# The experts' first product of units 8 to 15 as 2x2 blocks with seven products, in a three-stage kernel on one Trainium2 core

## The chip, the core and the metric

The kernel runs on one core of one Trainium2 chip. The core has five engines that run side by side, each through its own instructions in order: TensorE (PE, with the loading of its stationary operand as PEld), VectorE (DVE), ScalarE (ACT), GpSimd (POOL) and SyncE (SP), which here only issues DMAs. Work on one engine waits for another's by semaphores. Matmul results go to PSUM, which PE writes and DVE and ACT read. The metric is device time in microseconds (us), the median of three runs.

## The reference

Three stages, each feeding the next, all in float32 (cut to what is computed):

```python
# 1. attention, 2 x 8 heads, 576 tokens, head size 64: a window of 32 keys, for half
#    the heads at a stride of 4; its output is x, 1152 tokens x 512
# 2. four experts, 512 -> 1024 -> 512
p = domain_probs / (domain_probs.sum(-1) + 1e-9)
for e in range(4):
    h = maximum(x @ w1[e], 0)
    out += p[:, e:e+1] * (h @ w2[e])
# 3. one layer 512 -> 2048 -> 512, its weights given in 64 bits
h = out @ w_in
P = a0 + a1*h + a2*h**2 + a3*h**3
Q = 1 + |b0|*|h| + |b1|*h**2
result = (P / (Q + 1e-6)) @ w_out
```

## The kernel before, in words

**Numbers in two parts.** Every operand of the large products is split in a high part (rounded to the matmul's own float32 form) and a low part (what the rounding lost), and a product is the sum of three: high times high, high times low, low times high.

**Units, chunks, groups.** The 1152 tokens are three chunks of 384 (TC). Hidden features are cut into units of 256; units 0 to 15 are the four experts, units 16 to 23 the last layer. Two units make a group g. An *h step* is the first product of one unit on one chunk: 2 blocks of 128 features, 4 pieces of the inner dimension, 3 products, so 24 matmuls of 128x128 by 128x384 (`h_bank`, line 321), into a PSUM tile of two banks. ACT then writes the relu's high part (`hh`, line 334) and DVE the low part (`hl`, line 335, which reads `hh`). An *o tile* is the second product of a group on 128 tokens: 12 matmuls of 512 columns (`o_half`, line 358) into one PSUM bank, and DVE multiplies it with the expert's weight and adds it to an accumulator in SBUF (`o_sum`, *acc*, line 382). There are three two-bank tiles for h steps, used in turn, and two banks for o tiles, `pso`; a bank is written again when what was in it has been read. The high and low parts of the first product are held in SBUF, six buffers of each.

**Weights.** A unit's w1 and w2 are loaded by SP into one of four raw buffers and split by `split_w` (lines 91 to 109): for each half, ACT casts 128x512 (line 105) and DVE subtracts (line 106). The split tiles come from one pool of four per name.

**Conversion.** Beside this, `convert` (lines 119 to 172) turns the 64-bit words of the last layer's weights into high and low parts, in 32 pieces of 128x512. A piece's words are loaded one piece ahead. ACT first takes a magnitude (line 143); then DVE works in six steps: t (line 145); t again (line 150); e and f (lines 155, 158); f plus t (line 162); a masking of f by the magnitude (line 165), which ACT copies into w (line 168); and the low part w (line 170), which reads ACT's copy, with the store of the piece to DRAM (line 171). The last layer loads from there. A generator yields after each step, and `pump(n)` puts the next n steps into the instruction streams; two sets of buffers alternate.

**Order.** The order of instructions on each engine is the order in which the code issues them; nothing reorders it. Attention comes first, with twelve units interleaved by hand. In the expert layer a group's order is: the h steps of both units on one chunk, then three o tiles; this for the chunks 0, 1, 2, the o tiles being those of the chunk before (of group g - 1 ahead of chunk 1's). Each h step and each o tile is followed by `pump(2)`. The splits and loads of the coming group's weights stand between them: `split_w1` before the h steps of chunk 1, `split_w2` before those of chunk 2. The last layer has no conversion; its activation is a longer chain on ACT and DVE.

Of the kernel before, what the change touches and what calls it, by code (L numbers as in the profile page):

```python
# [33 lines left out]
TC = 384  # L35
# [3 lines left out]
NG1, NG = 2 * E, 2 * E + F2 // 512  # L39
QSCALE = 1.0 / D ** 0.5  # L40
# [4 lines left out]
def body(ctx, tc, qkv, mask, dp, w1, w2, w1d, w2d, coef, out):  # L45
# [5 lines left out]
    wp = ctx.enter_context(tc.tile_pool(name="wp", bufs=4))  # L51
    dram = ctx.enter_context(tc.tile_pool(name="dram", bufs=1, space=DRAM))
    rawp = ctx.enter_context(tc.tile_pool(name="rawp", bufs=4))
# [11 lines left out]
    mask_sb = const.tile([128, 4, 320], BF16, name="mask_sb")  # L65
# [11 lines left out]
    w1s, w2s, scratch = {}, {}, {}  # L77
# [12 lines left out]

    def split_w(store, nm):
        raws = {}

        def split(u, halves=(0, 1)):
            if u >= 2 * NG1:
                return
            if halves[0] == 0:
                raws[u] = store[u]
                store[u] = wp.tile([128, 2, 1024], F32R, tag=nm, name=nm)
            raw, w = raws[u], store[u]  # L100
# [13 lines left out]
    def weight(store, u, n):  # L114

        return (store[u][:, i].rearrange("p (k f) -> p k f", k=n) for i in range(2))


    def convert(pool):
# [15 lines left out]
        for n, (_, dst, s) in enumerate(pieces):  # L135
# [4 lines left out]
            f = pool.tile([128, 512], F32, tag="f", name="f")  # L140
# [198 lines left out]

    def rows(t):  # L340
# [130 lines left out]
    with tc.manual_schedule():  # L471
        attn_pool, x_pool = tc.tile_pool(name="attn", bufs=3), tc.tile_pool(name="psx", bufs=1, space=PSUM)
        ap, psx = attn_pool.__enter__(), x_pool.__enter__()
# [50 lines left out]
        for n, f in enumerate(then):  # L524
# [7 lines left out]
            9: [lambda: split_w2(3), lambda: load_w1(5)],  # L532
# [131 lines left out]
        attn_pool.__exit__(None, None, None)  # L664
        third.append(ctx.enter_context(tc.tile_pool(name="psh3", bufs=1, space=PSUM)))
        conv_pool = tc.tile_pool(name="conv", bufs=2)
        steps = convert(conv_pool.__enter__())
# [6 lines left out]
        def h_step(u, c):  # L674
# [3 lines left out]
            if u < 2 * NG1:  # L678
                h_relu(u, c, ps)
                pump()  # L680
# [27 lines left out]
        for g in range(NG):  # L708
            u = 2 * g
            if g == 0:  # L710
                h_step(0, 2)
                h_step(1, 2)
                o_step(0, 2)
                continue
            more = g + 1 < NG
            if g == NG1:
                for _ in steps:
                    pass
                conv_pool.__exit__(None, None, None)
# [16 lines left out]
            elif g > 1:  # L736
# [4 lines left out]
            if g == 1:  # L741
                load_w2(u + 2)
                load_w2(u + 3)
                extra = {0: [(split_w1, u + 2)], 2: [(split_w1, u + 3)]}
            elif more:
                split_w1(u + 2)
                load_w2(u + 2)
            if g > 1:
                h_step(u, 1)
# [3 lines left out]
            if g > 1 and more:  # L753
                split_w1(u + 3)
                load_w2(u + 3)
            if g > 1:
                h_step(u + 1, 1)
# [3 lines left out]
            if more:  # L761
                split_w2(u + 2)
# [3 lines left out]
            if more:  # L766
                split_w2(u + 3)
# [3 lines left out]
            if g == NG1 - 1:  # L771
                x2_half(0, 0)
                x2_half(0, 1)
# [151 lines left out]
```

## Time and profile before

| | |
|---|---|
| median of three runs | 653.68 us (652.66 to 653.69) |
| profiled execution, its own time | 652.89 us |
| its span, first to last instruction | 650.9 us |
| busy: PE, PEld | 639.6 us (98%), 574.6 us (88%) |
| busy: DVE | 485.0 us (75%) |
| busy: ACT, POOL | 277.7 us (43%), 17.0 us (3%) |
| DMA, mean over the span | 122 GB/s |

The profile is one execution. Busy time of PE counts a matmul from its start to its modelled end, and matmuls overlap in the pipeline, so the time that one costs in a row of them is the distance of two starts, which is less than its listed duration. In the chain of waits, a row is a stretch of work on one engine that the end of the program hung on; the next row is what followed it without anything else coming later. The expert layer goes from about 87 to 420 us, and in it the chain's rows alternate between first products (line 321) and second products (line 358). An "idle time" is time that an engine stood still before an instruction, put down to the event that came last.

### The profile page before, as it was taken

The page shows a single profiled execution, that of the slowest core. Times are in us where ns is not written, and L with a number is a line of the kernel's source. Part 1 is how long each engine was busy: PE and PEld are TensorE (multiplying, and loading weights), DVE is VectorE, ACT ScalarE, POOL GpSimd, SP SyncE. Part 2 cuts the span into 40 slices and gives each one's busy share as a digit, 9 for nine tenths or more (in the row PEclk, how much of TensorE's full clock was granted, in tenths as well). Part 3 has the DMA queues.
Part 4 walks back from the last instruction along what each step waited for, and adds up shares of the span by engine and source line. Part 5 has one row for each costly group of instructions (what it writes and reads, how often), then busy time and mean ns, then how long its engine had stood idle before and what let it go on. Part 6 is the DMA issues. An engine that isn't in the chain of part 4 may idle for free.

```text
span 650.9 us, 9488 instructions
## 1 busy us (share of the span) xinstructions
PE 639.6 (98%) x3838; PEld 574.6 (88%) x3839; DVE 485.0 (75%) x693; ACT 277.7 (43%) x518; POOL 17.0 (3%) x30
## 2 busy tenths in 40 slices
PE   8989999999999999999999999999999999999996
PEld 4878898999999999999999999989999999999985
DVE  6767326867867777777767766436999999999986
ACT  5887412413313323223233232115666555556651
POOL 2311100000000000000000000000000000000000
PEclk9999999999999999999999999999999999999999
DMA  9973011545344444454553572431230330300012
GB/s 293 275 219 104 21 65 47 195 148 172 120 161 149 142 163 137 154 162 115 176 162 102 161 254 93 167 130 38 92 130 1 129 130 2 129 1 1 0 49 97
DMA packets 25707, 79.53 MB, mean 122 GB/s; under 512 B 2720, under 2 KB 3232, under 8 KB 23616
## 3 DMA queue, kind: packets, MB, share of 16 engines
q1 hardware_dynamic: 25376, 78.77, 37.4%
q8 instruction: 30, 0.49, 0.3%
q10 hardware_dynamic: 288, 0.16, 0.1%
q14 instruction: 13, 0.11, 0.0%
HBM read 59.79 MB, written 19.14 MB: 121 GB/s over the span
## 4 chain that ended last, share of the span: by engine, by line
PE 94%; DVE 3%; ACT 2%; issue 0%; DVEq 0%; ACTq 0%
PE ps_h L321 46%; PE ps_o L358 43%; PE ps_v L285 1%; ACT pr L250 1%; PE ps_s L271 1%; PE ps_s L218 1%; PE ps_h L403 1%; PE ps_h L547 1%; PE ps_h L358 0%; DVE u L447 0%; DVE acc L388 0%; DVE u L460 0%; DVE sq L455 0%; DVE sq L452 0%; DVE sq L437 0%
## 5 line engine op out<-in xcount | busy, mean ns | idle before, releaser
L321 PE MATMUL ps_h<-xh,w 128*128 128x384 f32 x1152 | 301.7, 336 | 2.0 <-DVE hl L335 2.0
L358 PE MATMUL ps_o<-w,hh 128*128 128x512 f32 x832 | 224.3, 391 | 0.0
L321 PEld LDWEIGHTS ps_h<-xh,w 128*128 128x128 f32 x1152 | 208.8, 188 | 3.9 <-DVE hl L335 2.2
L321 PE MATMUL ps_h<-xl,w 128*128 128x384 f32 x576 | 192.7, 335 | 0.0
L358 PEld LDWEIGHTS ps_o<-w,hh 128*128 128x128 f32 x832 | 155.1, 188 | 31.1 <-ACT hh L334 0.4
L358 PE MATMUL ps_o<-w,hl 128*128 128x512 f32 x416 | 128.6, 390 | 0.0
L321 PEld LDWEIGHTS ps_h<-xl,w 128*128 128x128 f32 x576 | 108.1, 188 | 1.2
L335 DVE SCALAR_TENSOR_TENSOR hl<-ps_h,hh 128x768 fp32r<-128x768 f32 x48 | 45.9, 957 | 73.2 <-ACT hh L334 73.2
L358 PEld LDWEIGHTS ps_o<-w,hl 128*128 128x128 f32 x416 | 78.0, 188 | 16.9 <-DVE hl L335 0.4
L334 ACT ACTIVATE hh<-ps_h 128x768 fp32r<-128x768 f32 x48 | 39.1, 814 | 120.6 <-PE ps_h L321 120.5
L168 ACT CAST w<-f 128x512 fp32r<-128x512 f32 x32 | 19.9, 621 | 123.6 <-DVE f L165 123.6
L382 DVE SCALAR_TENSOR_TENSOR acc<-ps_o,p_sb,acc 128x512 f32<-128x512 f32 x63 | 47.1, 748 | 11.4 <-PE ps_o L358 11.4
L106 DVE TENSOR_TENSOR w<-raw,w 128x512 fp32r<-128x512 f32 x64 | 42.0, 695 | 0.7 <-ACT w L105 0.6
L170 DVE TENSOR_TENSOR w<-f,w 128x512 fp32r<-128x512 f32 x32 | 22.2, 692 | 22.8 <-ACT w L168 22.8
L441 ACT ACTIVATE ab<-sq,cbias 128x768 f32<-128x768 f32 x24 | 22.6, 944 | 37.2 <-DVE sq L437 37.0
L105 ACT CAST w<-raw 128x512 fp32r<-128x512 f32 x60 | 34.0, 617 | 0.0
L432 ACT ACTIVATE sq<-ps_h 128x768 f32<-128x768 f32 x24 | 19.3, 803 | 32.4 <-PE ps_h L321 32.4
L250 ACT ACTIVATE pr<-pr,mx 128x80 f32<-128x80 f32 (+1 forms) x84 | 29.7, 356 | 6.5 <-DVE mx L243 6.3
L437 DVE SCALAR_TENSOR_TENSOR sq<-sq,absb,ab 128x768 f32<-128x768 f32 x24 | 24.3, 1011 | 3.8 <-ACT ab L433 3.8
L467 DVE TENSOR_TENSOR hl<-u,hh 128x768 fp32r<-128x768 f32 x24 | 22.9, 954 | 5.4 <-ACT hh L464 5.4
L447 DVE SCALAR_TENSOR_TENSOR u<-u,na,ps_h 128x768 f32<-128x768 f32 x24 | 24.3, 1014 | 0.9
L460 DVE SCALAR_TENSOR_TENSOR u<-u,na,sq 128x768 f32<-128x768 f32 x24 | 24.3, 1013 | 0.4
(64 smaller groups left out, 521.0 us busy)
## 6 DMA issues: line engine op xcount, KB each, us to landing
w<-w SPq DMA_DIRECT2D x32, 512.0 KB, 3.6
w<-w SPq DMA_DIRECT2D x16, 1024.0 KB, 5.4
raw<-in_w_dram SPq DMA_DIRECT2D x30, 512.0 KB, 5.9
x<-in_w1d_dram SPq DMA_DIRECT2D x16, 512.0 KB, 5.1
x<-in_w2d_dram SPq DMA_DIRECT2D x16, 512.0 KB, 5.2
out_dram<-acc SPq DMA_DIRECT2D x8, 256.0 KB, 2.2
v<-in_qkv_dram SPq DMA_DIRECT2D x6, 320.0 KB, 6.7
qk<-in_qkv_dram SPq DMA_DIRECT2D x4, 448.0 KB, 5.3
```

Source lines behind the costliest of these rows:

```text
L105: (nc.vector.tensor_copy if early else nc.scalar.copy)(w[:, 0, s], raw[:, s])
L106: nc.vector.tensor_tensor(out=w[:, 1, s], in0=raw[:, s], in1=w[:, 0, s].bitcast(F32), op=ALU.subtract)
L250: nc.scalar.activation(pr[:, j, i], pr[:, j, i], AF.Exp, scale=-1.0, bias=self.mx[:, j, i:i + 1], accum_out=self.total[:, j, i:i + 1],)
L321: nc.tensor.matmul(ps[:, i, :TC], lhsT=a[:, k, f], rhs=b[:, k], start=k + n == 0, stop=k + n == 5,)
L334: nc.scalar.activation(hh, ps[:, :, :TC], AF.Relu)
L335: nc.vector.scalar_tensor_tensor(out=hl, in0=ps[:, :, :TC], scalar=0.0, in1=hh.bitcast(F32), op0=ALU.max, op1=ALU.subtract,)
L358: nc.tensor.matmul(ps, lhsT=a[:, i, tk], rhs=b[:, i], start=v + n == 0, stop=v + n == 6)
L382: nc.vector.scalar_tensor_tensor(out=acc[t], in0=ps, scalar=pe, in1=acc[t], op0=ALU.mult, op1=ALU.add)
L437: nc.vector.scalar_tensor_tensor(out=self.sq, in0=self.sq, scalar=absb[:, 1:2], in1=self.ab, op0=ALU.mult, op1=ALU.add,)
L447: nc.vector.scalar_tensor_tensor(out=self.u1, in0=self.u1, scalar=na[:, 1:2], in1=ps, op0=ALU.add, op1=ALU.mult)
L460: nc.vector.scalar_tensor_tensor(out=self.u1, in0=self.u1, scalar=na[:, 0:1], in1=self.sq, op0=ALU.add, op1=ALU.mult)
L467: nc.vector.tensor_tensor(out=self.hl, in0=self.u1, in1=self.hh.bitcast(F32), op=ALU.subtract)
```

## The change

Units 8 to 15 (groups 4 to 7) compute their first product on chunks 1 and 2 another way; chunk 0 stays an h step. Take the two feature blocks (f) against the two chunks (c), and the inner dimension in two halves (k). That is a product of two 2x2 matrices of blocks, and it is formed with seven block products in place of eight (the scheme of Strassen and Winograd). Each block product is 2 pieces of the inner dimension times 3 products, 6 matmuls of 128x384 as before; a unit's two chunks take 42 of them where they took 48.

What goes with it:

- `sum_w1(u)`: four sums of blocks of w1, on DVE (four 128x256 additions), and their split (a 128x1024 cast on ACT, a 128x1024 subtraction on DVE), into a tile `w1t` of the pool `wp1`.
- `sum_x()`: the four sums of half chunks of x, once, in twelve DVE operations of 128x768 and four casts on ACT, given out two at a time behind o tiles of group 3.
- `Blocks`: the products accumulate in the four banks of two h tiles, `c11`, `m`, `c12`, `p`. After the first product ACT writes its negation into `m` (line 441), and after the second ACT copies `p` to SBUF (line 444). `half` (line 450) and `most` (line 461) are two DVE operations of 128x384 that read `m` and the copy and write the banks `c12` and `p`. The methods `first`, `second` and `third` issue the products; the last product goes on top in bank `m`.
- The order of all groups from 0 to 7 is written anew: one unit after the other, with its o tiles between its h steps (`plain` for groups 2 and 3, `blocks` for 4 to 7). Conversion steps come three at a time behind h steps and o tiles of the opening and of group 2, two in group 3, and in the block groups 26 a group, some ahead of `half` and `most`.
- Pools: w1 and w2 get pools of their own (four and three tiles), raw buffers go from four to three, and the conversion's magnitude is put into `w[:, 1]` and its f into e.
- The load of the fourth w1 moves behind a split of the first, the split of the fourth w2 out of attention into the opening.

The diff, cut to its core ("..." where lines are left out):

```diff
+NBLOCK = 4
...
     xp = ctx.enter_context(tc.tile_pool(name="xp", bufs=1))
     hp = ctx.enter_context(tc.tile_pool(name="hp", bufs=6))
-    wp = ctx.enter_context(tc.tile_pool(name="wp", bufs=4))
+    wp1 = ctx.enter_context(tc.tile_pool(name="wp1", bufs=4))
+    wp2 = ctx.enter_context(tc.tile_pool(name="wp2", bufs=3))
...
                 return
             if halves[0] == 0:
-                raws[u] = store[u]
-                store[u] = wp.tile([128, 2, 1024], F32R, tag=nm, name=nm)
-            raw, w = raws[u], store[u]
+                raws[nm, u] = store[u]
+                store[u] = pools[nm].tile([128, 2, 1024], F32R, tag=nm, name=nm)
+            raw, w = raws[nm, u], store[u]
...
+    wts = {}
+    def sum_w1(u):
+        raw = raws["w1", u].rearrange("p (k f) -> p k f", k=4)
+        a, b, c, d = (raw[:, k:k + 2, f:f + 128] for f in (0, 128) for k in (0, 2))
+        t = sump.tile([128, 4, 2, 128], F32, tag="t", name="t_w")
+        for i, (x, y) in enumerate(((c, d), (a, c), (t[:, 0], a), (t[:, 2], b))):
+            nc.vector.tensor_tensor(out=t[:, i], in0=x, in1=y, op=ALU.add)
+        wts[u] = w = wp1.tile([128, 2, 1024], F32R, tag="w1", name="w1t")
+        t = t.rearrange("p i k f -> p (i k f)")
+        nc.scalar.copy(w[:, 0], t)
+        nc.vector.tensor_tensor(out=w[:, 1], in0=t, in1=w[:, 0].bitcast(F32), op=ALU.subtract)
...
-            mag = pool.tile([128, 512], F32, tag="mag", name="mag")
+            f = e.bitcast(F32)
             w = pool.tile([128, 2, 512], F32R, tag="w", name="w")
+            mag = w[:, 1].bitcast(F32)
             nc.scalar.activation(mag, high.bitcast(F32), AF.Abs)
             nc.vector.tensor_scalar(
...
+    def product(ps, a, b, first=False):
+        (wh, wl), (xh, xl) = a, b
+        for k in range(2):
+            for n, (w, x) in enumerate(((wh, xh), (wh, xl), (wl, xh))):
+                nc.tensor.matmul(
+                    ps, lhsT=w[:, k], rhs=x[:, k],
+                    start=first and k + n == 0, stop=k + n == 3, skip_group_check=not first,
+                )
+    ssum = {}
+    def sum_x():
+        sh = sxp.tile([128, 4, 2, TC], F32R, tag="sh", name="sh")
+        sl = sxp.tile([128, 4, 2, TC], F32R, tag="sl", name="sl")
...
+        def whole(c, half):
+            xh, xl = (t[:, 2 * half:2 * half + 2].bitcast(F32) for t in xt[c])
+            t = tmp.tile([128, 2, TC], F32, tag="m", name="x_w")
+            nc.vector.tensor_tensor(out=t, in0=xh, in1=xl, op=ALU.add)
+            return t
+        def less(i, a, b, out):
+            nc.vector.tensor_tensor(out=out, in0=a, in1=b, op=ALU.subtract)
+            nc.scalar.copy(sh[:, i], out)
+        def low(i, t):
+            nc.vector.tensor_tensor(out=sl[:, i], in0=t, in1=sh[:, i].bitcast(F32), op=ALU.subtract)
+        x11 = whole(1, 0)
+        yield
+        x12 = whole(2, 0)
+        yield
+        less(0, x12, x11, x11)
+        yield
...
+    class Blocks:
...
+        def __init__(self, u):
+            self.u = u
+            w = [t.rearrange("p (k f) -> p k f", k=4) for t in (w1s[u][:, 0], w1s[u][:, 1])]
+            ws = [wts[u][:, i].rearrange("p (n k f) -> p n k f", n=4, k=2) for i in range(2)]
+            self.block = lambda f, k: [t[:, 2 * k:2 * k + 2, f * 128:(f + 1) * 128] for t in w]
+            self.sums = lambda n: [t[:, n] for t in ws]
+            self.x = lambda c, k: [t[:, 2 * k:2 * k + 2] for t in xt[c]]
+            self.t = lambda n: [ssum[i][:, n] for i in "hl"]
+        def first(self):
+            self.ps = h_tile(), h_tile()
+            (c11, m), (c12, p) = ([t[:, i, :TC] for i in range(2)] for t in self.ps)
+            self.banks = c11, m, c12, p
+            product(c11, self.block(0, 0), self.x(1, 0), True)
+            nc.scalar.mul(m, c11, -1.0)
+            product(p, self.sums(0), self.t(0), True)
+            self.p = tmp.tile([128, 2, TC], F32, tag="m", name="m_p")[:, 0]
+            nc.scalar.copy(self.p, p)
+            product(c11, self.block(0, 1), self.x(1, 1))
+            product(m, self.sums(2), self.t(1))
+        def half(self):
+            c11, m, c12, p = self.banks
+            nc.vector.scalar_tensor_tensor(
+                out=c12, in0=m, scalar=-1.0, in1=self.p, op0=ALU.mult, op1=ALU.subtract
+            )
+        def second(self):
+            c11, m, c12, p = self.banks
+            product(m, self.sums(1), self.t(2))
+            product(c12, self.sums(3), self.x(2, 1))
+        def most(self):
+            c11, m, c12, p = self.banks
+            nc.vector.tensor_tensor(out=p, in0=m, in1=self.p, op=ALU.add)
+        def third(self):
+            product(self.banks[1], self.block(1, 1), self.t(3))
...
         units[1].split()
-        load_w1(3)
         units[3].exps((1,))
         run(6)
         split_w1(0, (1,))
+        load_w1(3)
         turn(2)
         units[3].norm()
...
+        def o_one(g, t, n=0):
+            o_tile(g, t)
+            pump(n)
+        h_step(0, 2)
+        h_step(1, 2)
+        for t in range(6, 9):
+            o_one(0, t, 3)
+        split_w1(4)
+        h_step(2, 2)
+        split_w2(3)
+        load_w2(4)
+        h_step(3, 2, 3)
+        for t in range(3):
+            o_one(1, t, 3)
+        split_w1(5)
+        xsteps = sum_x()
...
+        def o_plain(g, t, n):
+            o_one(g, t, 3 if n == 3 else 1)
+            if n == 2:
+                next(xsteps, None)
+                next(xsteps, None)
+        def plain(g):
             u = 2 * g
-            if g == 0:
-                h_step(0, 2)
-                h_step(1, 2)
-                o_step(0, 2)
-                continue
+            n = 3 if g + 1 < NBLOCK else 2
+            h_step(u, 0, n)
+            for t in range(3, 6):
+                o_plain(g - 1, t, n)
+            split_w2(u)
+            load_w2(u + 1)
+            h_step(u, 1, n)
+            load_w1(u + 2)
+            for t in range(6, 9):
+                o_plain(g - 1, t, n)
+            h_step(u, 2, n)
+            split_w2(u + 1)
+            load_w2(u + 2)
+            h_step(u + 1, 0, n)
+            load_w1(u + 3)
+            split_w1(u + 2)
+            h_step(u + 1, 1, n)
+            if g + 1 == NBLOCK:
+                sum_w1(u + 2)
+            o_plain(g, 0, n)
+            h_step(u + 1, 2, n)
+            for t in range(1, 3):
+                o_plain(g, t, n)
+            split_w1(u + 3)
+        def blocks(g):
+            u = 2 * g
+            h_step(u, 0, 0)
+            split_w2(u)
+            load_w2(u + 1)
+            o_one(g - 1, 3)
+            o_one(g - 1, 4)
+            b = Blocks(u)
+            b.first()
+            pump(2)
+            b.half()
+            o_one(g - 1, 5, 3)
+            b.second()
+            pump(2)
+            b.most()
+            o_one(g - 1, 6, 3)
+            sum_w1(u + 1)
+            b.third()
+            h_relu(u, 1, b.ps[0])
+            load_w1(u + 2)
+            o_one(g - 1, 7, 2)
+            o_one(g - 1, 8)
+            h_relu(u, 2, b.ps[1])
+            split_w1(u + 2)
+            h_step(u + 1, 0, 0)
+            split_w2(u + 1)
+            load_w2(u + 2)
+            b = Blocks(u + 1)
+            b.first()
+            load_w1(u + 3)
+            pump(2)
+            b.half()
+            o_one(g, 0, 3)
+            b.second()
+            pump(2)
+            b.most()
+            o_one(g, 1, 3)
+            if u + 2 < 2 * NG1:
+                sum_w1(u + 2)
+            b.third()
+            h_relu(u + 1, 1, b.ps[0])
+            o_one(g, 2, 4)
+            h_relu(u + 1, 2, b.ps[1])
+            split_w1(u + 3)
+        for g in range(2, NG1):
```

**DVE in the opening, behind the second o tile of the expert layer's third run of them** (conversion: t, e, f, w are tiles of a piece, x its words; acc is an o tile's accumulation; line numbers are those of each kernel). Before, three steps stand between two acc at the one place and two at the other:

```order
L382 SCALAR_TENSOR_TENSOR acc_1153<-ps_o,p_sb,acc_1153 128x512
L155 TENSOR_SCALAR e<-t 128x512
L158 SCALAR_TENSOR_TENSOR f<-x_1472,e 128x512
L162 TENSOR_TENSOR f<-f,t 128x512
L382 SCALAR_TENSOR_TENSOR acc_1178<-ps_o,p_sb,acc_1178 128x512
L165 SCALAR_TENSOR_TENSOR f<-mag,f 128x512
L170 TENSOR_TENSOR w<-f,w 128x512
L382 SCALAR_TENSOR_TENSOR acc_1212<-ps_o,p_sb,acc_1212 128x512
```

After:

```order
L508 SCALAR_TENSOR_TENSOR acc_1154<-ps_o,p_sb,acc_1154 128x512
L163 TENSOR_SCALAR t<-x_1584 128x512
L168 SCALAR_TENSOR_TENSOR t<-x_1584,t 128x512
L173 TENSOR_SCALAR e<-t 128x512
L176 SCALAR_TENSOR_TENSOR e<-x_1584,e 128x512
L508 SCALAR_TENSOR_TENSOR acc_1179<-ps_o,p_sb,acc_1179 128x512
L180 TENSOR_TENSOR e<-e,t 128x512
L183 SCALAR_TENSOR_TENSOR e<-w,e 128x512
L188 TENSOR_TENSOR w<-e,w 128x512
L508 SCALAR_TENSOR_TENSOR acc_1213<-ps_o,p_sb,acc_1213 128x512
```

Between two acc now stand three steps of a piece (four instructions, where e and f belong to one step), before two.

**ACT at unit 9** (hh is a relu, the casts of raw are splits of w2 tiles, the cast of e or f and the copy of a magnitude belong to the conversion). Before, around the same place in its work:

```order
L105 CAST w_2599<-raw 128x512 x2
L334 ACTIVATE hh<-ps_h 128x768
L143 ACTIVATE mag<-x_2554 128x512
L105 CAST w_2645<-raw 128x512 x2
L334 ACTIVATE hh<-ps_h 128x768
L168 CAST w<-f 128x512
L143 ACTIVATE mag<-x_2635 128x512
```

After:

```order
L352 ACTIVATE hh<-ps_h 128x768 x2
L109 CAST w_2667<-raw 128x512 x2
L352 ACTIVATE hh<-ps_h 128x768
L109 CAST w_2701<-raw 128x512 x2
L441 ACTIVATE ps_h<-ps_h 128x384
L444 COPY m_p<-ps_h 128x384
L186 CAST w<-e 128x512
```

The negation of the first block product (line 441) and the copy of the second (line 444) stand behind the relu of the unit's chunk 0 and the two casts of its w2.

**DVE in the block of unit 10.** Before, two hl with a piece's steps between them:

```order
L335 SCALAR_TENSOR_TENSOR hl<-ps_h,hh 128x768
L155 TENSOR_SCALAR e<-t 128x512
L158 SCALAR_TENSOR_TENSOR f<-x_2406,e 128x512
L162 TENSOR_TENSOR f<-f,t 128x512
L335 SCALAR_TENSOR_TENSOR hl<-ps_h,hh 128x768
L165 SCALAR_TENSOR_TENSOR f<-mag,f 128x512
L170 TENSOR_TENSOR w<-f,w 128x512
L382 SCALAR_TENSOR_TENSOR acc_1382<-ps_o,p_sb,acc_1382 128x512
```

After, from `half` (line 450) to `most` (line 461):

```order
L450 SCALAR_TENSOR_TENSOR ps_h<-ps_h,m_p 128x384
L508 SCALAR_TENSOR_TENSOR acc_1213<-ps_o,p_sb,acc_1213 128x512
L168 SCALAR_TENSOR_TENSOR t<-x_2801,t 128x512
L173 TENSOR_SCALAR e<-t 128x512
L176 SCALAR_TENSOR_TENSOR e<-x_2801,e 128x512
L180 TENSOR_TENSOR e<-e,t 128x512
L183 SCALAR_TENSOR_TENSOR e<-w,e 128x512
L188 TENSOR_TENSOR w<-e,w 128x512
L461 TENSOR_TENSOR ps_h<-ps_h,m_p 128x384
```

The two operations in PSUM stand one acc and five conversion steps apart; ACT's copy into w lies between the last two of these steps.

## Rows read from the trace of the kernel before

**Rows 1.** The page, parts 1 and 2: busy us, share, instructions; granted clock.
```profile
PE 639.6 (98%) x3838; PEld 574.6 (88%) x3839; DVE 485.0 (75%) x693; ACT 277.7 (43%) x518; POOL 17.0 (3%) x30
...
PEclk9999999999999999999999999999999999999999
```

**Rows 2.** Chain that ended last: start us, length us, what; from the opening.
```profile
120.31 8.34 PE ps_h L321 x48
128.65 8.20 PE ps_o L358 x36
```

**Rows 3.** One group: length; busy us, instructions of PE, PEld, DVE, ACT, POOL.
```profile
136.85:186.49 49.64, 49.64 (x254) 45.30 (x253) 37.05 (x59) 14.96 (x24) 0.00 (x0) 1.00 0.46 149
```

**Rows 4.** DVE's waits in five groups: total us, times, longest.
```profile
DVE hl L335 <- ACT hh L334: 39.8, 25, 3.2
DVE w L170 <- ACT w L168: 18.5, 26, 0.7
DVE acc L382 <- PE ps_o L358: 2.8, 15, 0.2
```

**Rows 5.** DVE in order of time: start us, us, operation [idle before <-releaser].
```profile
100.67 0.96 DVE L335 SCALAR_TENSOR_TENSOR hl<-ps_h,hh 128x768 fp32r<-128x768 f32 x1 [3.20 <-ACT hh L334]
...
104.83 0.96 DVE L335 SCALAR_TENSOR_TENSOR hl<-ps_h,hh 128x768 fp32r<-128x768 f32 x1 [2.14 <-ACT hh L334]
105.70 0.42 DVE L155 TENSOR_SCALAR e<-t 128x512 uint32<-128x512 uint32 x1
106.15 0.69 DVE L158 SCALAR_TENSOR_TENSOR f<-x,e 128x512 f32<-128x512 uint32 x1
106.88 0.69 DVE L162 TENSOR_TENSOR f<-f,t 128x512 f32<-128x512 f32 x1
107.49 0.74 DVE L380 TENSOR_SCALAR acc<-ps_o,p_sb 128x512 f32<-128x512 f32 x1
108.15 0.68 DVE L165 SCALAR_TENSOR_TENSOR f<-mag,f 128x512 f32<-128x512 f32 x1
109.52 0.69 DVE L170 TENSOR_TENSOR w<-f,w 128x512 fp32r<-128x512 f32 x1 [0.69 <-ACT w L168]
110.13 0.74 DVE L380 TENSOR_SCALAR acc<-ps_o,p_sb 128x512 f32<-128x512 f32 x1
```

**Rows 6.** DVE again: a split and the next step.
```profile
121.14 1.28 DVE L106 TENSOR_TENSOR w<-raw,w 128x512 fp32r<-128x512 f32 x2
122.34 0.42 DVE L155 TENSOR_SCALAR e<-t 128x512 uint32<-128x512 uint32 x1
```

**Rows 7.** Groups by shape: count | busy us, mean ns of one | idle before.
```profile
L321 PE MATMUL ps_h<-xh,w 128*128 128x384 f32 x1152 | 301.7, 336 | 2.0 <-DVE hl L335 2.0
...
L106 DVE TENSOR_TENSOR w<-raw,w 128x512 fp32r<-128x512 f32 x64 | 42.0, 695 | 0.7 <-ACT w L105 0.6
...
L105 ACT CAST w<-raw 128x512 fp32r<-128x512 f32 x60 | 34.0, 617 | 0.0
...
L467 DVE TENSOR_TENSOR hl<-u,hh 128x768 fp32r<-128x768 f32 x24 | 22.9, 954 | 5.4 <-ACT hh L464 5.4
...
L306 ACT CAST xh<-ps_v 128x384 fp32r<-128x384 f32 x10 | 6.1, 614 | 5.6 <-PE ps_v L285 5.6
...
L507 DVE TENSOR_TENSOR p_sb<-dp_sb,psum_sb 128x36 f32<-128x36 f32 x1 | 0.2, 198 | 0.0
```

**Rows 8.** ACT in order of time: a split's casts, a relu, the next.
```profile
127.54 1.14 ACT L105 CAST w<-raw 128x512 fp32r<-128x512 f32 x2
128.69 0.82 ACT L334 ACTIVATE hh<-ps_h 128x768 fp32r<-128x768 f32 x1
129.40 0.66 ACT L143 ACTIVATE mag<-x 128x512 f32<-128x512 f32 x1
```

**Rows 9.** A piece's words (tile x): DMA issue to landing.
```profile
DMA to landing us min/median/max: 3.7/5.2/6.8
```

**Rows 10.** The store of a piece (line 171): issue to landing.
```profile
DMA to landing us min/median/max: 3.1/3.6/4.9
```

More of the change, by code (lines that the diff above doesn't have):

```diff
@@ L97, in split @@
             if halves[0] == 0:
-                raws[u] = store[u]
-                store[u] = wp.tile([128, 2, 1024], F32R, tag=nm, name=nm)
-            raw, w = raws[u], store[u]
+                raws[nm, u] = store[u]
+                store[u] = pools[nm].tile([128, 2, 1024], F32R, tag=nm, name=nm)
+            raw, w = raws[nm, u], store[u]
             for i in halves:
@@ L338, in h_relu @@
         )
+    def product(ps, a, b, first=False):
[10 more added lines that the diff above has]
+        sl = sxp.tile([128, 4, 2, TC], F32R, tag="sl", name="sl")
+        ssum.update(h=sh, l=sl)
+        def whole(c, half):
[14 more added lines that the diff above has]
+        yield
+        x22 = whole(2, 1)
+        yield
+        low(0, x11)
+        yield
+        less(2, x12, x22, x12)
+        yield
+        nc.vector.tensor_tensor(out=x22, in0=x22, in1=x11, op=ALU.subtract)
+        nc.scalar.copy(sh[:, 1], x22)
+        yield
+        low(2, x12)
+        yield
+        x21 = whole(1, 1)
+        yield
+        low(1, x22)
+        yield
+        less(3, x21, x22, x21)
+        yield
+        low(3, x21)
+        yield
@@ L664, in body @@
         attn_pool.__exit__(None, None, None)
+        mask_pool.__exit__(None, None, None)
         third.append(ctx.enter_context(tc.tile_pool(name="psh3", bufs=1, space=PSUM)))
-        conv_pool = tc.tile_pool(name="conv", bufs=2)
-        steps = convert(conv_pool.__enter__())
+        early = [tc.tile_pool(name=n, bufs=b) for n, b in (("tmp", 3), ("sump", 1), ("sxp", 1), ("conv", 2))]
+        tmp, sump, sxp, conv = (p.__enter__() for p in early)
+        steps = convert(conv)
         between, pairs = [], []
@@ L706, in o_step @@
                     f()
-        for g in range(NG):
-            u = 2 * g
-            if g == 0:
-                h_step(0, 2)
-                h_step(1, 2)
-                o_step(0, 2)
-                continue
+        def o_one(g, t, n=0):
+            o_tile(g, t)
+            pump(n)
+        h_step(0, 2)
[7 more added lines that the diff above has]
+        h_step(3, 2, 3)
@@ L715, in body @@
+        for g in range(2, NG1):
+            (plain if g < NBLOCK else blocks)(g)
+        u = 2 * g
+        o_tile(g, 3)
+        x2_half(0, 0)
+        x2_half(0, 1)
+        o_tile(g, 4)
+        o_tile(g, 5)
+        load_w1(u + 4)
+        load_w1(u + 5)
+        for g in range(NG1, NG):
+            u = 2 * g
             more = g + 1 < NG
@@ L718, in body @@
                     pass
-                conv_pool.__exit__(None, None, None)
+                for p in early[::-1]:
+                    p.__exit__(None, None, None)
                 Rational.pool = ctx.enter_context(tc.tile_pool(name="rat", bufs=3))
@@ L735, in body @@
                 r2.numerator()
-            elif g > 1:
+            else:
                 h_step(u, 0)
@@ L740, in body @@
             extra = {}
-            if g == 1:
+            load_w2(u + 1)
+            if more:
                 load_w2(u + 2)
[L743 to L749, printed above, removed]
+            h_step(u, 1)
             if g == NG1:
@@ L752, in body @@
                 extra = {0: [(x2_turn, 2, 1), (x2_split, 2, 0), (x2_split, 2, 1)]}
[L753 to L757, printed above, removed]
+            h_step(u + 1, 1)
             if g == NG - 1:
```

22 lines of the change are left out of this document (7 added, 15 removed).

## The prediction

> **What bounds the kernel now.** [...] Then the chain of waits [rows 2]: in the expert layer it is PE alone, blocks of 48 matmuls of 384 columns (8.34 us, 173.8 ns each) and of 36 matmuls of 512 columns (8.20 us, 227.8 ns each), one behind the other without a gap. So in this stage a matmul taken out saves its start-to-start time, as long as nothing makes PE wait. Who could? A group of two units takes PE 49.64 us; DVE is busy 37.05 of them, ACT 14.96 [rows 3]. DVE's waits over five such groups (248.2 us) [rows 4] tell how much of its idle time is free: 39.8 + 2.8 us wait for results of PE, 8.5 us per group. The other 18.5 us (3.7 per group) lie inside conversion pieces, where DVE stands still for ACT's copy; they are as good as work. DVE is a second bound, 8.5 us in 49.64 away.
>
> **Prices.** From start to start in DVE's rows [rows 5]: a tensor_scalar (t, e) 0.45; a 512-wide two-input operation 0.61 before a stranger (106.88 to 107.49), 0.73 before one that reads it (106.15 to 106.88); the masking step 1.37 up to w, because ACT's copy lies between; w 0.61; an acc 0.66; an hl 0.87. A split of one weight tile is 1.20 [rows 6]. A conversion piece pumped in pairs of steps is 0.45+0.61+0.45+0.73+0.61+1.37+0.61 = 4.83 us; in threes two more results are read at once, 4.95. Check on a group of before: 30 steps are 5 pieces, 24.2, with 6 hl 5.2, 9 acc 5.9 and 4 splits 4.8 that is 40.1, which leaves 9.5 free where 8.5 was measured. The prices are, if anything, low.
>
> **What the change takes out.** In each of units 8 to 15, chunks 1 and 2 take 7 products of 6 matmuls where they took 48 matmuls: 6 fewer, 48 in all, and the shape, 128x384, is one that the rows show. 48 x 173.8 ns = 8.34 us. The profiled execution took 652.89 (span 650.9); the median of the runs, 653.68, is 0.79 more. With nothing lost the median would become 645.3.
>
> **What it adds, stage by stage.**
> *Ahead of the blocks (A).* The opening (4 h steps, 6 o tiles) is the same PE work as before up to 128.65 [rows 2]. DVE starts in it with the hl of 100.67 and stands 2.14 us before the next [rows 5]; 4 hl 3.5, 6 acc 4.0, 3 splits 3.6 and 27 steps 22.0 then end at 135.9, 7.2 us behind PE. Lag alone hurts nobody; due points do. There are two o banks, so an o tile starts only when the acc of the tile two earlier is done, and a matmul starts 0.16 us before the last one ends (336 ns long [rows 7], 174 apart). The third o tile behind the first h step of group 2 is due at 128.65+4.17+5.47-0.16 = 138.13. DVE has its acc at 135.9 + hl 0.87 + 3 steps 2.48 + 0.75 = 140.0: 1.9 us late. Up to the same point of the next run DVE has 12 steps 9.9, 3 acc 2.0, a split 1.2, an hl 0.87, 13.95 us in all, and PE 4.17+8.20 = 12.37: 3.5 late. On to the end of group 2 there are 30 steps, 5 acc, 4 hl and 3 splits, 35.1, and DVE ends at 189.0 where PE, unmoved, ends at 178.3. Group 3 has fewer steps, but the twelve 768-wide operations of the chunk sums, two behind an o tile, each counted like an hl (0.954 long [rows 7]): the same points come out 4.5 and 5.4 us late. PE never makes up a wait, so the latest counts: A = 5.4.
> *Inside a block (B).* Between the o tile that follows the negation and the last product PE has 12 matmuls and one o tile, 2.09+2.73-0.16 = 4.66 us. In that time DVE does an acc 0.66, three steps, two steps, and the add in PSUM that the last product waits for (384 wide; by the line through 512 and 768 wide 0.56 [rows 7]). By the conversion's phase the five steps are 3.58 us (units 8, 9, 14, 15), 4.62 (10, 11) or 3.77 (12, 13), so the product is 0.14, 1.18 or 0.33 late, and B = 4 x 0.14 + 2 x 1.18 + 2 x 0.33 = 3.6.
> *The negation on ACT (C).* PE comes back to the first bank 12 matmuls after the h step, 2.09-0.16 = 1.93 us. In each second unit ACT has first the relu (0.71 to its next start), the two casts of a w2 split (1.15) [rows 8] and the 384-wide negation (0.61, as the cast of that width [rows 7]), 2.47: 0.54 late, four times, C = 2.2. In first units two o tiles lie between, and nothing is late.
> *What is left on DVE (D).* A block group has 26 steps 21.2, hl, acc and splits 16.0, four adds in PSUM 2.1, and two weight sums. Of a sum the rows show no 256-wide add: it lies between 0.198 (36 wide) and 0.695 (512 wide) [rows 7]; I take 0.44, on the line through 512 and 768. Four of them less overlap 1.5, the wait for ACT's 1024-wide cast 1.2 (twice a 512-wide one at most [rows 7]) and a 1024-wide subtract 1.2 are 3.9. Together 47.1 of PE's 47.55 us: no room where 8.5 were, and each wait of DVE that the order forces goes to PE. The nearest row is the 2.8 us behind o tiles in five groups [rows 4]; I take 2.5, between 0 and 8 (32 adds at the upper bound).
> Sum: -8.34+5.4+3.6+2.2+2.5 = +5.4: 658.2 for a profiled run, 659.0 for the median.
>
> [...]
>
> At no cost I put four edits. The chunk sums' four casts run on ACT, which is two thirds idle; the cover is gone only at C. Loads from three raw buffers: the closest has two o tiles before its split and an h step behind it, so only one later than 9.6 us would hold a relu. The fourth w1 load now waits on SP behind a split of the first weight, with other loads behind it, in the attention stage; its own split comes two attention units later, and if that cover fails the first relus of unit 3 slip. The second layer keeps its order but for one o tile and two loads.
>
> **Rivals.**
> 1. *DVE keeps up and the gain stays.* For it: PE waits for DVE nowhere in this stage now, and if DVE's prices are 4% high, A falls by more than half and B with it. Then 8.34 less 0 to 4.7: 645.3 to 650. Against it: the check above, which has them low.
> 2. *Only the block's own waits.* A needs a lag that builds over 100 us and shows only at the o banks; if DVE's order leaves it 3% more room there, A and D are small, while B and C, fixed inside each block, stay: 653.68-8.34+5.8 = 651.1, from 650 to 653.
> 3. *Transfers on top, slower still.* A piece's words land 5.2 us after issue, 6.8 at most, its store 3.6, at most 4.9 [rows 9, 10], and they are asked for one piece ahead: in before three pumps of 49.64/15 us each, 9.9, but two o tiles, 5.5, in a run of them with three steps each. The magnitude also moves into the result tile, so ACT's first step of a piece waits for the store of two pieces back, with relus queued behind it and PE behind them. At 0.5 us for each of the 12 pieces of opening and group 2 that is 6 us on top: 665. It decides where a piece lasts less than issue, landing and store together.
> PE's order has 42 matmuls where 48 stood, so that the change isn't made is no case.
>
> **Chances.** Forecast 0.60 (656 to 663.5), rival 1 0.17, rival 2 0.13, rival 3 0.10. About 0.2%, 1.3 us, can be told from no change. Rival 1 is faster, rival 2 faster or, in its upper half, the same, the rest slower: faster 0.24, same 0.07, slower 0.69. The range, 650 to 666, leaves out rival 1 and the far end of rival 3.
>
> **What would show it.** Six matmuls fewer per unit at the same 174 ns; PE's o tiles waiting for DVE's acc in groups 2 and 3, some 5 us together; PE waiting for the add in PSUM before each last product, longest in units 10 and 11; PE waiting for ACT's negation in second units alone; DVE over 85% busy from 130 to 420 us, its waits for relus mostly gone. I am wrong if PE's blocks stay without gaps, if these waits come to under 8 us, or if the longest of them are for DMA.

## The result, and the profile after

The changed kernel takes 661.68 us (660.40 to 663.26, four runs) against 653.67 before: 1.0127 times as long, 95% interval 1.0098 to 1.0157. Forecast was 659.0 in a range from 650 to 666: slower, by 5.3 us; it was 8.0. The four runs lie in two pairs, 660.40 and 660.60 us at a mean granted clock of 0.999 and 1.000, 662.76 and 663.26 at 0.997 and 0.996, so a gain counted from their median is uncertain by about 1 us.

The profiled execution is of the longer pair, 662.76 us (span 660.7), 9.87 more than that of before. Most of this lies in the expert stage: from its first row of first products (87.28 us before, 88.33 after) to the row of 48 first products with which the last layer goes on (440.04 and 449.96) it is 352.76 us before and 361.63 after, 8.87 longer. This length leaves out what the attention stage does, and the experiments below are compared by it as well. The page, parts 1 and 2 as in [rows 1]:

```profile
PE 638.7 (97%) x3791; PEld 566.4 (86%) x3791; DVE 522.1 (79%) x761; ACT 293.6 (44%) x546; POOL 17.0 (3%) x30
...
PEclk9989999999999999999999999999999999999999
```

PE has 47 matmul records fewer than before, and yet the span is longer: the time is in waits. PE's waits from 87 to 440 us (total us, times, longest); in before the same view is empty:

```profile
PE ps_o L484 <- DVE acc L508: 4.5, 5, 1.4
PE ps_h L365 <- ACT ps_h L441: 3.4, 5, 1.8
PE ps_h L365 <- DVE ps_h L461: 2.7, 4, 1.2
```

These are the three kinds that the prediction named: o tiles for an acc (A), the second product of c11 for ACT's negation (C), the last product for the add in PSUM (B). But 10.6 us is only the idle time. PE's rows (start us, length us) around one wait of each kind show what a wait costs:

```profile
139.34 0.61 PE L484 MATMUL ps_o<-w,hl 128*128 128x512 f32 x2
141.30 0.50 PE L484 MATMUL ps_o<-w,hh 128*128 128x512 f32 x1 [1.34 <-DVE acc L508]
...
269.43 0.34 PE L365 MATMUL ps_h<-sh,w1t 128*128 128x384 f32 x1
271.54 0.44 PE L365 MATMUL ps_h<-xh,w 128*128 128x384 f32 x1 [1.77 <-ACT ps_h L441]
...
307.14 0.61 PE L484 MATMUL ps_o<-w,hl 128*128 128x512 f32 x2
308.91 0.44 PE L365 MATMUL ps_h<-sh,w 128*128 128x384 f32 x1 [1.15 <-DVE ps_h L461]
309.19 0.34 PE L365 MATMUL ps_h<-sl,w 128*128 128x384 f32 x1
```

Without the wait the last product would have begun 2 x 0.2278 us after 307.14, at 307.60; it began at 308.91, 1.31 later, 0.16 more than the idle time, because matmuls overlap. And the next matmul follows after 0.28 instead of 0.174. So a wait costs its idle time and some 0.27 us more, of which the prediction's due points, set 0.16 us ahead of a matmul's end, hold the first part. From the starts of all matmuls, by the same reckoning:

| | predicted | measured |
|---|---|---|
| 48 matmuls fewer | -8.34 | -8.34 |
| A, o banks (127.3, 141.3, 155.3, 193.2, 207.2 us) | 5.4 | 5.9 |
| B, add in PSUM, eight units | 3.6 | 5.0 |
| C, negation, units 9, 10, 11, 13, 15 | 2.2 | 4.7 |
| D, other waits for DVE | 2.5 | none |
| later start of the stage (PE's clock at 38.5 us) | - | 1.0 |
| more switches between kinds of matmul | - | 0.9 |
| sum (the two executions differ by 9.87) | 5.4 | 9.2 |

The two lines ahead of the sum are read below (the last section, and e6); 0.7 us stay without a name.

### The profile page after: what moved, and what is told of

The parts are those of the page before. It is cut to its first block, busy times and chain, and to the rows that moved or that the text cites. A ratio compares the mean times of both kernels' runs of the same rounds, so it can differ in the third digit from the quotient of the medians.

```text
span 660.7 us, 9464 instructions
## 1 busy us (share of the span) xinstructions
PE 638.7 (97%) x3791; PEld 566.4 (86%) x3791; DVE 522.1 (79%) x761; ACT 293.6 (44%) x546; POOL 17.0 (3%) x30
## 4 chain that ended last, share of the span: by engine, by line
PE 65%; DVE 23%; ACT 7%; issue 3%; DMA 1%; SPq 0%; DVEq 0%; ACTq 0%
PE ps_o L484 29%; PE ps_h L339 26%; PE ps_h L365 6%; DVE acc L508 2%; DVE e L183 2%; DVE hl L353 2%; ACT pr L268 2%; ACT w L186 2%; DVE t L168 2%; DVE e L180 2%; DVE w L188 2%; DVE w L110 2%; DVE e L176 1%; PE ps_v L303 1%; ACT w L109 1%
## 5 line engine op out<-in xcount | busy, mean ns | idle before, releaser
L339 PE MATMUL ps_h<-xh,w 128*128 128x384 f32 x896 | 236.8, 337 | 1.8 <-DVE hl L353 1.8
L339 PEld LDWEIGHTS ps_h<-xh,w 128*128 128x128 f32 x896 | 162.9, 188 | 3.7 <-DVE hl L353 2.1
L339 PE MATMUL ps_h<-xl,w 128*128 128x384 f32 x448 | 150.3, 335 | 0.0
L339 PEld LDWEIGHTS ps_h<-xl,w 128*128 128x128 f32 x448 | 84.3, 188 | 1.1
L186 ACT CAST w<-e 128x512 fp32r<-128x512 f32 x32 | 19.9, 621 | 146.1 <-DVE e L183 146.1
L188 DVE TENSOR_TENSOR w<-e,w 128x512 fp32r<-128x512 f32 x32 | 22.1, 689 | 15.1 <-ACT w L186 15.1
L365 PE MATMUL ps_h<-sh,w1t 128*128 128x384 f32 x96 | 28.6, 338 | 0.0
```

Of the source, the lines that this page charges most:

```text
L186: nc.scalar.copy(w[:, 0], f)
L188: nc.vector.tensor_tensor(out=w[:, 1], in0=f, in1=w[:, 0].bitcast(F32), op=ALU.subtract)
L339: nc.tensor.matmul(ps[:, i, :TC], lhsT=a[:, k, f], rhs=b[:, k], start=k + n == 0, stop=k + n == 5,)
L365: nc.tensor.matmul(ps, lhsT=w[:, k], rhs=x[:, k], start=first and k + n == 0, stop=k + n == 3, skip_group_check=not first,)
```

## The experiments

The theory after the comparison, called that of places: each kind of wait is made by what stands ahead of a due instruction in DVE's or ACT's queue, and there is an order in which nothing is late, so that the 8.34 us can be had. The rivals: DVE has no room for the work at all; or the blocks are to blame and not the order.

**e1, no blocks.** Groups 4 to 7 run `plain(g)`; the blocks and the weight sums are gone, the rest stays:

```diff
-            o_one(g, t, 3 if n == 3 else 1)
+            o_one(g, t, 3 if n == 3 else 1 if g + 1 < NBLOCK or t > 5 and g + 1 == NBLOCK else 2)
...
-            if g + 1 == NBLOCK:
-                sum_w1(u + 2)
...
         for g in range(2, NG1):
-            (plain if g < NBLOCK else blocks)(g)
+            plain(g)
```

> Groups 4 to 7 in the plain order, with full h steps in place of the 2x2 blocks (48 matmuls more; no weight sums; two steps behind each h step and o tile there). The rest, three steps a place in the opening and group 2 and the chunk sums in group 3, stays. Theory of places (the loss sits at named waits: 5.9 us for o banks ahead of the blocks, 1.05 in attention, some 10 in the blocks): before plus 7.0, 660.5 median. Rival, that the blocks themselves lose all of it: 653.7, as before.

Measured: 660.69 (ratio to before 1.0119, 1.0094 to 1.0143). PE's waits in the stage:

```profile
PE ps_o L484 <- DVE acc L508: 4.8, 5, 1.4
```

The loss of A is made before the place where the first block would begin. The waits cost 6.2 us by the starts of the matmuls, and the stage is 359.56 us long, 6.8 more than before. The forecast's other term, 1.05 in the attention stage, is not in this trace: the granted clock is 1.00 from 26 to 46 us, and the stage begins at 87.47. That the median comes this close to 660.5 is partly luck. Blocks and plain h steps come out within some 2 us of each other: what the blocks save in matmuls they lose in their own waits.

**e2, the add ahead of its steps**, in both places:

```diff
             b.second()
-            pump(2)
             b.most()
+            pump(2)
```

> The two conversion steps ahead of the add in PSUM (line 461) stand behind it, in all eight units. Theory of places: the 5.2 us at the last product go, 656.5. Rival, that DVE has no room in the block groups, so the two steps come late at the next acc, relu or half: 660 to 662, with new waits for acc.

Measured: 659.15 (1.0090, 1.0073 to 1.0107), 2.5 less than the changed kernel where 5.2 were expected; the stage is 358.20 us long, 3.4 less. B is gone from the list, a new wait is in it:

```profile
PE ps_o L484 <- DVE acc L508: 4.4, 5, 1.4
PE ps_h L365 <- ACT ps_h L441: 2.6, 4, 0.9
PE ps_h L365 <- DVE hl L353: 1.4, 2, 1.2
```

DVE now comes late to an hl, which holds the h tile of the next block. Neither side was quite right: the place costs what it was said to, but with DVE already behind a part of it comes up again elsewhere.

**e3, the negation ahead of the w2 split** in second units:

```diff
-            split_w2(u + 1)
-            load_w2(u + 2)
             b = Blocks(u + 1)
             b.first()
+            split_w2(u + 1)
+            load_w2(u + 2)
```

> In second units the split of w2 (two casts on ACT) stands behind the block's first products instead of ahead of the negation. Theory of places: of 5.2 us at the second product of c11 in odd units all goes but some 1.0 at unit 9, where a load of w1 came late: 657.5 to 658. Rival, that ACT's delay only moves to the second product of w2 or to DVE: over 660.

Measured: 658.82 (1.0083, 1.0063 to 1.0103), 2.9 less than the changed kernel where 3.7 to 4.2 were expected; the stage is 358.14 us long, 3.5 less. (The 5.2 of the forecast is 4.1 by the table's reckoning: C without unit 10.) One wait for the negation is left, at unit 10, a first unit, which the move does not touch:

```profile
PE ps_o L484 <- DVE acc L508: 4.8, 5, 1.3
PE ps_h L365 <- DVE ps_h L461: 2.5, 3, 1.1
PE ps_h L365 <- ACT ps_h L441: 0.4, 1, 0.4
```

**e4, two steps a place** in the opening and group 2. This kernel leaves out the arithmetic of the last four pieces:

```diff
+            if n >= 28:
+                nc.sync.dma_start(dst[:, :, s], w.bitcast(F32))
+                yield
+                continue
...
-            o_one(0, t, 3)
+            o_one(0, t, 2)
...
-        h_step(3, 2, 3)
+        h_step(3, 2, 2)
...
-            o_one(g, t, 3 if n == 3 else 1)
+            o_one(g, t, 2 if n == 3 else 1)
...
+            m, n = n, 2
```

> Two conversion steps a place instead of three in the opening and group 2; to keep the number of steps elsewhere, the arithmetic of the last four pieces is left out (their stores send the last converted tile). Theory of places: the o banks' waits in the opening, groups 2 and 3 (5.9 us, and nothing later) go, 655.8. Rival, that the chunk sums of group 3 hold the o banks by themselves: 2 us of it stay, 658.

Measured: 658.22 (1.0081, 1.0062 to 1.0100), 3.5 less, not 5.9; the stage is 357.93 us long, 3.7 less. A fell to one wait, in group 3, where the chunk sums stand, but B grew:

```profile
PE ps_h L369 <- DVE ps_h L465: 5.0, 6, 1.2
PE ps_h L369 <- ACT ps_h L445: 2.4, 4, 1.0
PE ps_o L488 <- DVE acc L512: 0.6, 1, 0.6
```

With 22 steps fewer ahead of the blocks, other steps of a piece fall between `half` and the add; four units now meet the phase with ACT's copy in it (1.2 us late), where two did. That most of A is the steps' doing is shown, and that a wait taken out at one place does not come back whole.

**e5, the three moves together**, as in e2, e3 and e4, the last four pieces' arithmetic left out again:

> The three moves of the last runs together: add ahead of its two steps, negation ahead of the w2 split, two steps a place in the opening and group 2 (the last four pieces' arithmetic left out). If each move's gain were its own: 661.7 less 2.5, 2.9 and 3.5, 652.8. By the theory that DVE's lag is one account from 100 us on: a step that no longer stands ahead of the add or the o bank stands ahead of an hl, so waits of products for hl and acc remain, some 5 to 7 us in all, and the time is 652 to 653 all the same, as much as before and not 8 less. If DVE had room to spare: 646.

Measured: 652.12 (0.9977, 0.9967 to 0.9986), as the theory had it and just below before, though with less arithmetic than before. The waits left:

```profile
PE ps_h L369 <- DVE hl L357: 2.2, 2, 1.1
PE ps_h L369 <- ACT ps_h L445: 0.6, 1, 0.6
PE ps_o L488 <- DVE acc L512: 0.6, 1, 0.6
```

By the starts of the matmuls they cost 5.2 us, within the 5 to 7 of the forecast. The time does not tell the theory from the sum of the three gains, which was forecast at 652.8, and in the length of the stage the three gains do add up: 3.4, 3.5 and 3.7 are 10.6, and here the stage is 350.99 us long, 10.6 less than in the changed kernel. So in sum the three moves neither help nor hinder each other, and of the three forecasts only 646 is ruled out.

**e6, steps by room.** All 192 steps, put where DVE stands idle: six ahead of the opening's first h step, where DVE waits for relus [rows 5]; the other counts were worked out by hand account from DVE's prices, so that no acc, hl, half or add is later than PE needs it; w2's split behind the negation:

```diff
-        h_step(0, 2)
...
+        OPEN_H, OPEN_O = (3, 1, 0, 1), (4, 4, 2, 3, 4, 2)
+        pump(6)
+        h_step(0, 2, OPEN_H[0])
...
             b.half()
-            o_one(g, 0, 3)
+            o_one(g, 0, 2)
             b.second()
-            pump(2)
             b.most()
+            pump(5)
-            o_one(g, 1, 3)
+            o_one(g, 1, 0)
```

> The whole computation, 192 steps. Steps are put where DVE stands idle: six ahead of the opening's first h step, 26 further in the opening, 37 in group 2, 27 in group 3, 24 in each block group, one to three of them between half and the add, none ahead of the add of second units, and the w2 split behind the negation. Theory of places: no PE wait of any length is left, and the 8.3 us of the 48 matmuls stay: 645 to 646.5. Rival, that DVE at 39 us busy and more in 47.6 leaves no order without waits: 650 or more.

Measured: 646.91 (646.48 to 647.43; 0.9898, 0.9884 to 0.9913), faster than both kernels, with the whole computation, and 0.4 above the forecast's upper end. One wait is left in the stage:

```profile
PE ps_o L484 <- DVE hl L353: 0.5, 1, 0.5
```

DVE had the room; the order did not use it. What lacks to 8.34 is read in the chain of waits (start us, us, what):

```profile
...
242.68 2.76 PE ps_o L484 x12
245.44 2.10 PE ps_h L365 x12
...
250.31 1.06 PE ps_h L365 x6
```

By the spacing of [rows 2] 12 matmuls of an o tile are 2.73 us, 12 of a product 2.09, 6 of one 1.04; each short stretch lasts 0.01 to 0.03 longer. Before, PE changed between the two kinds 40 times in this stage, now 78 times, as in the changed kernel: 38 x 0.025 is about 0.9. With the wait, 0.8 by the starts, that leaves 6.6 of the 8.34; 6.5 were measured, 6.2 in the length of the stage.

**e7, three steps in the kernel before**, its order untouched:

```diff
                 if g < NG1:
-                    pump()
+                    pump(3 if g < 2 or g == 2 and c < 2 else 2)
...
-                pump()
+                pump(3 if u in (4, 5) else 2)
```

> The kernel before, its order and computation untouched, with three conversion steps a place in the opening and group 2 (units 4 and 5), as the change has them there. Theory of places: o tiles wait for an acc two tiles earlier in the first groups as in the changed kernel, 5.5 to 6 us in all and none after group 2: 659. Rival, that the order by single units brings these waits: 653, as before.

Measured: 659.52 (1.0093, 1.0078 to 1.0109), with the same kind of wait:

```profile
PE ps_o L358 <- DVE acc L382: 5.1, 3, 2.2
```

So waits of A's kind need neither the blocks nor the order by units: in before, too, a third step a place is enough. The three waits cost 5.9 us by the starts of the matmuls, none of them after group 2.

**e8 and e9, one place each**, in the version of e6, where DVE is not behind. e8 puts the w2 split ahead of the block again (the edit of e3 the other way round), e9 five steps between `half` and the add (its edit against e6):

```diff
             b.half()
-            o_one(g - 1, 5, 1)
+            o_one(g - 1, 5, 3)
             b.second()
             pump(2)
             b.most()
-            pump(2)
...
             b.half()
-            o_one(g, 0, 2)
+            o_one(g, 0, 3)
             b.second()
+            pump(2)
             b.most()
-            pump(5)
+            pump(2)
```

> The version with steps by room, in which alone the w2 split of second units stands ahead of the block again, as in the change. Theory of places: the price of this one place, without any lag of DVE, is the prediction's 0.54 us and some 0.1 of restart in each of the four odd units: 2.2 to 2.6 more, 649.3, with PE waiting for ACT's negation four times and for nothing else. Rival, that these waits came from DVE's lag through ACT's queue: no change, 647.

> The version with steps by room, in which alone five conversion steps stand between half and the add in PSUM again, as in the change (the same number of steps in all). Theory of places: the add is late in every unit, by the phase of the conversion 0.2 to 1.2 us, and each wait costs some 0.3 more: 6 to 7 us, 653.4. Rival, that the steps cost where they stand in the change only because DVE was late already: 648 or less.

Measured: e8 648.85 (0.9934, 0.9919 to 0.9949), 1.9 more than e6; e9 652.54 (0.9995, 0.9986 to 1.0005), 5.6 more. Both are a little under their forecasts, 2.2 to 2.6 and 6 to 7, and far from the rivals'. The waits, beside the one of e6, e8 first:

```profile
PE ps_h L365 <- ACT ps_h L441: 0.9, 4, 0.2
```

```profile
PE ps_h L365 <- DVE ps_h L461: 3.6, 8, 0.7
```

Each place has its price without any lag: C four waits, once per odd unit, B eight. The two are 7.5 of the 8.34 us, with an idle time of only 4.5: the rest is, within 0.2, the 0.27 us at each of twelve waits.

## Why the prediction was right

**The direction and the mechanism** came from setting DVE's account against PE's due points, and that held. DVE's rows at the first due point of the forecast (as [rows 5]):

```profile
135.73 1.29 DVE L110 TENSOR_TENSOR w<-raw,w 128x512 fp32r<-128x512 f32 x2
136.93 0.95 DVE L353 SCALAR_TENSOR_TENSOR hl<-ps_h,hh 128x768 fp32r<-128x768 f32 x1
...
139.89 0.69 DVE L188 TENSOR_TENSOR w<-e,w 128x512 fp32r<-128x512 f32 x1 [0.69 <-ACT w L186]
140.50 0.75 DVE L508 SCALAR_TENSOR_TENSOR acc<-ps_o,p_sb,acc 128x512 f32<-128x512 f32 x1
```

The opening was to end at 135.9 on DVE and ended at 136.93, and this execution began the stage 1.05 us late, so it stood where it was said to. The acc is done at 141.25 (140.0 predicted, 1.05 of the difference being the late start). The loss there is 1.5 us where 1.9 was forecast, because PE had already lost 0.5 at 127.3, in the opening, where the forecast had no wait.

**A, 5.4 and 5.9.** Right in place, size and cause (e1, e4, e7). The five waits come to 5.3 us of lateness, as the latest due point had it; the rest is the slow step to the second matmul, five times. A lone wait in group 3 is left in e4, so the chunk sums have a small part in it, as forecast.

**B, 3.6 and 5.0.** Right: longest in units 10 and 11. There DVE goes from half to the add like this:

```profile
302.93 0.75 DVE L508 SCALAR_TENSOR_TENSOR acc<-ps_o,p_sb,acc 128x512 f32<-128x512 f32 x1 [1.36 <-PE ps_o L484]
303.60 0.68 DVE L168 SCALAR_TENSOR_TENSOR t<-x,t 128x512 uint32<-128x512 uint32 x1
304.32 0.43 DVE L173 TENSOR_SCALAR e<-t 128x512 uint32<-128x512 uint32 x1
304.78 0.69 DVE L176 SCALAR_TENSOR_TENSOR e<-x,e 128x512 f32<-128x512 uint32 x1
305.50 0.69 DVE L180 TENSOR_TENSOR e<-e,t 128x512 f32<-128x512 f32 x1
306.31 0.69 DVE L183 SCALAR_TENSOR_TENSOR e<-w,e 128x512 f32<-128x512 f32 x1
307.69 0.69 DVE L188 TENSOR_TENSOR w<-e,w 128x512 fp32r<-128x512 f32 x1 [0.69 <-ACT w L186]
308.30 0.56 DVE L461 TENSOR_TENSOR ps_h<-ps_h,m_p 128x384 f32<-128x384 f32 x1
```

The five steps take 4.70 us (303.60 to 308.30), predicted 4.62, and the product is 1.31 late, predicted 1.18; by the other two phases 0.19 and 0.38, predicted 0.14 and 0.33. That is 4.1 us in all. The other 0.9 is a price that was left out: the step to the second matmul after a wait, eight times 0.11. The expert stage of before had no waits to show it; its attention stage had one, at 37.74 us (0.277 to the second matmul).

**C, 2.2 and 4.7.** The mechanism was right in odd units (e3, e8). In units 13 and 15 the product is 0.39 and 0.36 late where 0.54 was forecast, since the negation is shorter than taken (0.41 to the next start, not 0.61); in unit 11, with DVE late, 0.99. Two waits failed the forecast. The sentence "in first units two o tiles lie between, and nothing is late" is wrong at unit 10. ACT there:

```profile
293.25 0.62 ACT L186 CAST w<-e 128x512 fp32r<-128x512 f32 x1 [5.34 <-DVE e L183]
293.77 0.81 ACT L352 ACTIVATE hh<-ps_h 128x768 fp32r<-128x768 f32 x1
294.48 1.13 ACT L109 CAST w<-raw 128x512 fp32r<-128x512 f32 x2
295.51 0.81 ACT L352 ACTIVATE hh<-ps_h 128x768 fp32r<-128x768 f32 x1
296.21 1.13 ACT L109 CAST w<-raw 128x512 fp32r<-128x512 f32 x2
297.24 0.49 ACT L441 ACTIVATE ps_h<-ps_h 128x384 f32<-128x384 f32 x1
```

ACT stood 5.34 us for DVE's masking step, with two relus, two splits and the negation queued behind. DVE's lag reaches PE through ACT's queue as well (0.5 us there). And at unit 9:

```profile
268.23 1.14 ACT L109 CAST w<-raw 128x512 fp32r<-128x512 f32 x2 [4.53 <-DMA raw<-in_w_dram]
269.28 0.80 ACT L352 ACTIVATE hh<-ps_h 128x768 fp32r<-128x768 f32 x1
...
271.01 0.48 ACT L441 ACTIVATE ps_h<-ps_h 128x384 f32<-128x384 f32 x1
```

The load is that of unit 10's w1. SP's rows around its issue (the last one holds three loads, of which it is the first):

```profile
259.43 0.52 SPq L189 DMA_DIRECT2D w<-w  x1
260.01 0.60 SPq L149 DMA_DIRECT2D x<-in_w1d_dram  x1
260.66 11.97 SPq L91 DMA_DIRECT2D raw<-in_w_dram  x3
```

It was not short of a raw buffer: it is issued before the last weight sum of unit 9 ends (261.20), and the load behind it, at 261.58, is the one that follows that sum. It stood in SP's queue behind the store of a conversion piece (259.43), which had waited for DVE's low part (done at 259.40), and behind the next piece's words. It landed 7.55 us after its issue, at 268.21, within the 9.6 us set as the bound: it was asked for late. So DVE's lag came to PE through SP's queue too, and the "loads from three raw buffers", costed at nothing, hold a relu and the negation once in this execution: 1.9 us, of which the place alone explains some 0.4. This is a small part of rival 3, in another place than it had named. The longest single wait of PE thus goes back to a DMA, close to the prediction's sign of being wrong ("if the longest of them are for DMA"); the next ones do not.

**D, 2.5 and nothing.** DVE's waits from 240 to 430 us in the changed kernel:

```profile
DVE acc L508 <- PE ps_o L484: 17.2, 9, 2.1
DVE hl L353 <- ACT hh L352: 3.3, 4, 1.4
```

In the block groups DVE had some 5 us of room each, not 0.4. The prices were some 4% high, 45.3 us a group where 47.1 were reckoned (49.0 of one group, less its 3.7 of waiting), and PE's waits under B and C lengthened the group. A term for "what is left" beside terms that slow PE counted the same time twice. Rivals 1 and 2 rested on this room, and it is there (e6); but it lies behind o tiles, not at the due points, so in the order of the change it is worth nothing. One sign failed with this term: DVE is busy 82% of the time from 130 to 420 us (238.8 of 290 us), not over 85%.

**The rest, and luck.** Of the four edits put at no cost, the raw loads are read under C. The last layer takes as long as before, within 0.1 us. Whether the moved load of the fourth w1 costs anything stays open (last section). The total is closer than its parts: the 2.5 us of D that did not come stood in for the 2.5 that C lacked, and 1.0 in the profile's sum is PE's clock, which the prediction did not have. What was right is the direction, the three waits and, for A and B, their places and sizes.

**A step that reads the one before.** Such steps take 0.72 (303.60 to 304.32, 304.78 to 305.50) and 0.81 (305.50 to 306.31), against 0.61 before a stranger (307.69 to 308.30): as in [rows 5], and more. The 0.72 and the 0.81 are no less than the 0.68 to 0.69 that an operation lasts in these rows, the 0.61 is less: here a step that reads the one before began after that one's end, the stranger ahead of it.

## What to carry to other kernels

When an edit takes work off the bounding engine and gives the second one more, write that engine's queue out between two due points, in start-to-start prices, and compare with the time until the result is needed; a busy share with room on average says nothing about a place (the changed kernel waited and had DVE room within the same group). Charge each wait about 0.3 us beside the idle time that a profile shows (0.27 here), and look through every queue between the late engine and the bound one, that of the DMAs included. Then put the deferrable work where the helper engine waits anyway: the same instructions took 661.7 us in one order and 646.9 in another.

## What was not expected of the hardware

A stall of PE costs more than its idle time: 0.16 us by the lost overlap and about 0.11 in the step to the second matmul (0.28 for 0.174, at 308.91 in the changed kernel). A short stretch of matmuls of one kind between two of the other lasts 0.01 to 0.03 us longer than its spacing says even without a wait (e6: 2.76 for 2.73).

In four profiles PE's granted clock falls for about 3 us in the attention stage: from 38.50 to 41.50 us it is 0.53 in the changed kernel and 0.50 in e4 and e7, from 38 to 42 us 0.62 in e5. From 38 to 42 us it is 1.00 in before, e1, e3 and e6; over the whole execution it is 0.999 in e2, 0.998 in e8 and 1.000 in e9. Two matmuls of 384 columns start 0.32 us apart in the changed kernel then (39.56 and 39.88), 0.18 in before (39.60 and 39.78). In the changed kernel's profile (length; busy us and count of PE, PEld, DVE, ACT, POOL; granted clock), against 1.00 in the same stretch of before:

```profile
38.50:41.50 3.00, 3.00 (x31) 2.34 (x29) 1.54 (x3) 3.00 (x17) 0.00 (x0) 0.53 0.75 228
```

PE had been busy for 2.16 of the 4 us from 34 to 38 in this execution and for 2.04 in that of before, where the clock did not fall. With it the expert stage begins 1.05 us later in this profile. e7 has it with before's own attention code, so it needs no part of the change; what decides it stays open. The start of the stage moves without it too: in e3, at a granted clock of 1.00, it comes 0.7 us later than before, and the chain of waits goes there through a load of a mask (11.3 us to its landing) and one of weights (9.9). Whether the moved load of the fourth w1 has a part in that, no run tells.
